# One conversion of the hidden layer is spread over three engines, and the order of all work is a new table

## The chip, the cores and the metric

The kernel runs on one core of a Trainium2 chip. The metric is the device time of one execution in microseconds (us). An execution has a span, from the first to the last instruction of the core, and a little time around it.

The core has five engines that run side by side, each with its own queue in a fixed order: TensorE (PE in the profile), VectorE (DVE), ScalarE (ACT), GpSimd (POOL) and SyncE (SP). SP issues nearly all DMAs here. An engine does nothing while the first instruction of its queue waits, so an instruction can be late because another one, ahead of it in the queue, waits for something else.

## The reference

```python
def _attn_ref(q, k, v, alpha):                 # all 4 x 8 x 768 x 48
    for t in range(S):
        state = alpha[:, :, t, :, None] * state + einsum('bhd,bhe->bhde', k[:, :, t], v[:, :, t])
        y[:, :, t] = einsum('bhd,bhde->bhe', q[:, :, t], state)

def _moe_ref(x, w_gate, w_val, w_out):         # x: 3072 x 384, hidden 1536
    g = x @ w_gate
    silu = g * (1.0 / (1.0 + exp(-g)))
    return (silu * (x @ w_val)) @ w_out
```

A gated linear recurrence over 768 steps per batch and head makes `y`; its heads side by side are the rows `x` of a gated feed-forward layer. The weights arrive in 64 bits.

## The kernel before, in words

**The recurrence** is cut into 16 units of 192 steps (4 batches x 4 units, names u = 0 to 15). For a unit, VectorE turns the loads of alpha, k and q (`tr`, `tk`, `tq`, line 399), runs a scan backwards (`G`, line 472) and one forwards (`f`, line 481), GpSimd or VectorE scale k and q (`mk`, `q`), and TensorE multiplies. From unit 4 on the products of a unit are one *burst* `Z` on TensorE: the outputs of the unit before (lines 658 to 680), the scores (line 565) and the carried state (line 584), some 3 us together. Before a burst, VectorE must have written the unit's `K` (`kr`, 16 transposes, line 540), and the unit's values must have been loaded (`V`, 8 DMAs, line 443). Behind the burst the output rows are split into two parts (`yh`, `yl`, lines 705 and 709) and ten DMAs (`xr`, line 745) lay them into `xT`, which the feed-forward reads. Units 0 to 3 are *turned* by TensorE instead (line 419).

**The feed-forward** is 96 steps: 8 blocks of 384 rows by 12 slices of 128 hidden columns. A block needs two units. TensorE keeps precision by three products of split operands, so each of a step's three parts is nine matmuls of 128x128 by 128x384: `g` and `v` (line 760), and `o` (line 793). Between them a step has a chain on the other engines: `sl`, the silu of `g`, on ScalarE (line 768); `h`, times `v`, on VectorE (line 772); `hh`, the upper part of `h`, a copy to the matmul's type on ScalarE (line 776); `hl`, the rest, `h - hh`, on GpSimd or VectorE (line 781). `g` has one PSUM bank, `v` one, and there are two buffers each of `h`, `hh` and `hl`.

Beside that the weights are converted in the first 140 us (lines 163 to 178, 343, 347), and later the weights and alpha are loaded once more for a check of their ranges (`wr`/`wc`, lines 300 and 303; `Lc`/`ck`, line 456).

**What sets the order.** The order of the whole program is written out in a table, `ORDER`, of 1637 words such as `v:h44` or `y:Lq11`: an engine (t TensorE, v VectorE, s ScalarE, g GpSimd, y SyncE) and a piece of work, for TensorE at times the PSUM banks. The last loop of `main_path` emits them in that order; each engine's queue holds its own words in it, and buffers are given out in it.

Of the kernel before, what the change touches and what calls it, by code (L numbers as in the profile page):

```python
# [49 lines left out]
t:Y0@36 s:yh0.0 y:La3 t:Ta2@20 s:pa3 s:ea2 y:Lk2 y:V1.0 s:w1a s:yh0.1 g:w1p y:Lq2 y:V1.3 y:V1.5 y:V1.2 v:w3v2 v:de1  # L50
t:S1@71 t:C1.0@2 s:ad1.0 v:yl0.0 v:ma1.2 t:Ta3@15 t:C1.1@4 s:ad1.1 t:C1.2@0 y:wl4 s:w4v0 s:ad1.2 g:pq2 g:pk2 g:vc1
v:ma1.1 v:yl0.1 v:ma1.0 t:Y1@64 s:yh1.0 v:w2v2 v:w2a s:yh1.1 t:R0.1@0 t:R0.2@3 t:Tq2@72 s:x0.2 s:x0.1 s:cq2 v:G2
v:yl1.0 v:yl1.1 t:R1.1@6 s:x1.1 v:w4v1 v:w4v2 t:Tk2@74 v:mk2 v:f2 v:q2 y:Lk3 s:pk3 t:R1.0@0 t:R0.0@6 y:V2.4 s:x0.0
s:x1.0 t:R1.2@7 s:x1.2 t:K2.0@2 s:kc2.0 g:w2p y:wl5 s:w5v0 y:V2.2 y:V2.0 y:Lq3 g:pq3 s:w4a t:Tk3@34 t:K2.1@7 s:kc2.1
t:g0 s:sl0 y:V3.1 y:V2.1 y:wl7 y:V2.3 y:V2.5 v:de2 g:vc2 g:lm0 y:V3.2 y:wl8 y:wl6 y:V3.3 y:V3.0 v:w5v1 s:ea3 v:G3
t:S2@20 s:qc2 v:ma2.2 v:mk3 v:ma2.0 v:lm1 y:wl11 y:wl9 y:V3.4 y:V3.5 s:w3a g:w3p g:w4p v:ma2.1 t:C2.0@7 t:K2.2@1
s:kc2.2 s:ad2.0 t:g1 t:v0 t:C2.1@3 v:h0 s:ad2.1 s:sl1 t:K3.0@7 s:kc3.0 t:Tq3@03 t:C2.2@1 s:ad2.2 s:cq3 s:hh0 s:w6v0
v:f3 t:v1 t:K3.1@7 t:g2 v:w5v2 g:hl0 v:h1 v:q3 v:de3 v:w6v1 s:hh1 s:kc3.1 s:sl2 t:Y2@20 s:yh2.0 v:hl1 v:w6v2 t:C3.0@4
t:S3@67 s:w5a g:w5p t:v2 s:ad3.0 t:C3.1@1 s:yh2.1 v:ma3.2 v:w8v0 v:yl2.0 s:w6a g:w6p t:o0 t:o1 v:ma3.1 v:yl2.1 y:wl12
y:La4 y:V4.5 y:wl10 s:w7v0 s:qc3 v:h2 v:ma3.0 y:xr2.0 y:xr2.1 v:w7v1 v:w7v2 v:w8v1 s:w9v0 s:ad3.1 s:vc3 t:g3 v:w8v2  # L60
v:w9v1 y:Lk4 y:wl13 y:xr2.2 t:Y3@20 s:sl3 s:w7a s:hh2 v:hl2 v:w7p s:w8a v:w8p s:yh3.0 s:yh3.1 t:v3 v:h3 s:w10v0 v:w9v2
s:hh3 v:hl3 t:g4 v:w10v1 s:sl4 s:w9a g:w9p t:o2 t:v4 v:yl3.1 v:yl3.0 v:h4 s:hh4 g:hl4 t:g5 v:w10v2 v:w10a s:w11v0
s:sl5 s:w12v0 t:v5 t:o3 v:w11v1 v:w10p t:g6 s:sl6 v:w12v1 v:w11v2 s:w11a v:h5 g:w11p s:hh5 t:o4 g:hl5 v:w12v2 y:xr3.0
y:xr3.1 y:xr3.2 y:wl16 y:V4.1 y:wl14 t:v6 v:tk4 v:h6 s:hh6 g:hl6 t:g7 v:tr4 v:G4 s:sl7 s:w13v0 s:w12a y:Lq4 v:mk4
# [1101 lines left out]
```

## Time and profile before

| | us |
|---|---|
| median of 3 runs | 547.37 (547.32 to 549.72) |
| the profiled execution | 549.81 |
| its span | 548.1 |
| TensorE busy in the span | 528.0 |
| VectorE, ScalarE, GpSimd busy | 400.5, 249.4, 151.2 |
| TensorE's granted clock | 0.999 (full speed, the 2.4 GHz level) |

The profile gives for each engine the time in which it is busy, and for an idle stretch what released it. Idle time of an engine is only worth something if TensorE's next matmul waits for it in the end. Matmuls are pipelined and their recorded ends are modelled, so TensorE's idle time is a lower bound of what it loses.

### The profile page before, as it was taken

What the parts mean: (1) busy time and instruction counts of PE and PEld (TensorE: products, weight loads), DVE (VectorE), ACT (ScalarE), POOL (GpSimd) and SP (SyncE); (2) the same over time, 40 slices, a digit from 0 to 9 for tenths busy, and PEclk for the clock granted to TensorE, in tenths of its full rate; (3) what the DMA queues carried; (4) which work ended last, traced back from release to release, by engine and by line L of the source; (5) the groups of instructions that cost most, each with busy time, mean ns of one, the idle gap of its engine ahead of it and who ended that gap; (6) DMA issues with size and microseconds to landing.
All of it is one profiled execution on the core that took longest, in us unless ns stands there. A gap on an engine that the chain in (4) does not pass through costs nothing.

```text
span 548.1 us, 13557 instructions
## 1 busy us (share of the span) xinstructions
PE 528.0 (96%) x5350; PEld 513.7 (94%) x5350; DVE 400.5 (73%) x755; ACT 249.4 (45%) x578; POOL 151.2 (28%) x149
## 2 busy tenths in 40 slices
PE   4899999999999999999989999999999999999996
PEld 3688999999999999999989999999899999999996
DVE  7999999999999998696798966889552674112122
ACT  5997655443222324533313533454533365454652
POOL 7245233545335222231313021031201030020100
PEclk9999999999999999999999999999999999999999
DMA  8989559456376547543634764255662315423511
GB/s 243 256 263 292 146 173 249 107 139 174 85 187 151 141 106 185 157 120 73 169 76 101 203 158 112 76 136 129 184 153 73 90 50 158 135 58 104 155 50 47
DMA packets 96195, 77.61 MB, mean 142 GB/s; under 512 B 33280, under 2 KB 93056, under 8 KB 96128
## 3 DMA queue, kind: packets, MB, share of 16 engines
q1 hardware_dynamic: 96048, 76.61, 52.3%
q8 instruction: 43, 0.70, 0.6%
q14 instruction: 24, 0.20, 0.1%
...
## 4 chain that ended last, share of the span: by engine, by line
PE 66%; DVE 3%; DMA 2%; SPq 1%; issue 1%; ACT 0%; POOL 0%; DVEq 0%; POOLq 0%
PE v L760 20%; PE ops L793 20%; PE g L760 20%; PE c L680 2%; PE s L565 1%; DMA L<-in_q_dram 1%; PE c L584 1%; PE y L658 1%; PE y L659 1%; DMA xT<-X 1%; SPq L745 1%; DMA V<-in_v_dram 1%; DVE h L772 0%; DVE V L629 0%; DVE K L540 0%
## 5 line engine op out<-in xcount | busy, mean ns | idle before, releaser
L760 PE MATMUL v<-xT,w 128*128 128x384 f32 x864 | 167.3, 337 | 0.6 <-DMA xT<-X 0.6
L760 PE MATMUL g<-xT,w 128*128 128x384 f32 x864 | 166.6, 336 | 0.6 <-ACT h L768 0.4
L793 PE MATMUL ops<-w,hh 128*128 128x384 f32 x576 | 158.5, 336 | 0.0
L760 PEld LDWEIGHTS v<-xT,w 128*128 128x128 f32 x864 | 150.5, 188 | 2.2 <-issue 0.9
L760 PEld LDWEIGHTS g<-xT,w 128*128 128x128 f32 x864 | 150.7, 188 | 1.8 <-ACT h L768 0.9
L781 POOL TENSOR_TENSOR hl<-h,hh 128x384 fp32r<-128x384 f32 x65 | 69.8, 1075 | 285.5 <-ACT hh L776 271.8
L772 DVE TENSOR_TENSOR h<-h,v 128x384 f32<-128x384 f32 x96 | 53.0, 552 | 89.9 <-PE v L760 61.6
L793 PEld LDWEIGHTS ops<-w,hh 128*128 128x128 f32 x576 | 105.5, 188 | 0.3
L768 ACT ACTIVATE h<-g 128x384 f32<-128x384 f32 x96 | 47.1, 490 | 119.6 <-PE g L760 101.0
L776 ACT CAST hh<-h 128x384 fp32r<-128x384 f32 x96 | 49.1, 511 | 112.0 <-DVE h L772 77.4
L793 PE MATMUL ops<-w,hl 128*128 128x384 f32 x288 | 96.8, 336 | 0.0
L540 DVE STREAM_TRANSPOSE K<-Gs 32x192 f32<-32x192 f32 x192 | 71.1, 370 | 3.3
L793 PEld LDWEIGHTS ops<-w,hl 128*128 128x128 f32 x288 | 54.0, 188 | 0.0
L347 POOL TENSOR_TENSOR w<-t,w 128x768 fp32r<-128x768 f32 (+1 forms) x15 | 27.5, 1842 | 34.4 <-ACT w L343 25.3
L781 DVE TENSOR_TENSOR hl<-h,hh 128x384 fp32r<-128x384 f32 x31 | 18.4, 594 | 22.8 <-ACT hh L776 22.7
L481 DVE TENSOR_TENSOR_SCAN AT<-AT,back 128x771 f32<-128x771 f32 x16 | 29.2, 1824 | 0.6
L606 DVE TENSOR_TENSOR X<-s,mask 64x384 f32<-64x384 f32 (+1 forms) x48 | 26.3, 551 | 3.8 <-PE s L565 3.1
L472 DVE TENSOR_TENSOR_SCAN Gs<-AT,inj 128x772 f32<-128x772 f32 x16 | 28.5, 1780 | 0.5 <-ACT AT L866 0.3
L497 POOL TENSOR_TENSOR X<-trq,AT 112x768 f32<-112x768 f32 x11 | 18.7, 1703 | 32.1 <-DMA xT<-X 11.0
L320 ACT ACTIVATE wc<-wc,wbias 128x384 f32<-128x384 f32 x36 | 23.3, 648 | 1.2
L629 DVE TENSOR_TENSOR V<-c,V 48x96 f32<-48x96 f32 x84 | 21.4, 255 | 2.8 <-ACT V L627 0.5
L893 POOL TENSOR_TENSOR Gs<-trk,Gs 128x768 f32<-128x768 f32 x9 | 15.3, 1700 | 26.0 <-DVE Gs L472 22.2
...
## 6 DMA issues: line engine op xcount, KB each, us to landing
...
```

The costliest lines, as they stand in the source:

```text
L320: nc.scalar.activation(dev, dev, AF.Relu, bias=wbias, scale=-1.0, accum_out=wviol[:, 0, i : i + 1])
L347: eng.tensor_tensor(out=lo, in0=src, in1=hi.bitcast(F32), op=ALU.subtract)
L472: nc.vector.tensor_tensor_scan(*(x.rearrange("p g t -> p (g t)")[:, ::-1] for x in (Gs, AT, inj)), 0.0, op0=ALU.mult, op1=ALU.add)
L481: nc.vector.tensor_tensor_scan(Af, Af, back[:, 1 : n + 1], back[:, 0:1], op0=ALU.mult, op1=ALU.add)
L540: nc.vector.transpose(out=bass.AP(k0.tensor, k0.offset, [k0.ap[0], (G * 2 * D, NU), (2 * D, GF), (1, 32)]), in_=Kg[j * BO + x : j * BO + x ...
L606: nc.vector.tensor_tensor(out=X[r, z, f * GF : (f + 1) * GF, :].rearrange("r g (c t) -> r g c t", c=NU), in0=sps[f][r].rearrange("r g (c t ...
L760: nc.tensor.matmul(pt, wsp[kind, f][a][:, kt * P : (kt + 1) * P], xT[blk][:, b_, kt, :], start=(n == 0), stop=(n == 3 * KT - 1),)
L768: nc.scalar.activation(h, acc.pop(("g", blk, f)), AF.Silu)
L772: nc.vector.tensor_tensor(out=h, in0=h, in1=acc.pop(("v", blk, f)), op=ALU.mult)
L776: nc.scalar.copy(out=hh, in_=acc["h", blk, f])
L781: eng.tensor_tensor(out=hl, in0=acc.pop(("h", blk, f)), in1=hh.bitcast(F32), op=ALU.subtract)
L793: nc.tensor.matmul(ops[blk][i], h[b_][:, i * P : (i + 1) * P], wsp["o", f][a], start=(first and n == 0), stop=(last and n == 2),)
```

## The change

`hh` takes an engine as an argument, and the table is another one. The number of words is the same, 1637; every matmul, load, store and check is still there.

| work (one instruction each) | before | after |
|---|---|---|
| `hh` | ScalarE 96 | ScalarE 45, GpSimd 30, VectorE 21 |
| `hl` | GpSimd 65, VectorE 31 | GpSimd 64, VectorE 32 |
| `mk` | GpSimd 9, VectorE 7 | GpSimd 6, VectorE 10 |
| `qc`, a copy of part of q | ScalarE 9, GpSimd 7 | ScalarE 7, GpSimd 6, VectorE 3 |

A few other words change their engine by one to three each (`q`, the conversions of weights, the copies of units 0 to 3). The table has one line less, so a line behind it has a number lower by one in the kernel after.

```diff
 ORDER = """
-s:first y:La0 s:pa0 t:Ta0@23 s:ea0 y:wl0 y:Lq0 s:pq0 v:w0v0 v:w0v1 v:w0v2 v:G0 v:f0 t:Tq0@03 v:q0 y:La1 s:pa1 t:Ta1@72
...
+s:first y:La0 s:pa0 t:Ta0@23 s:ea0 y:wl0 y:Lq0 s:pq0 t:Tq0@03 v:w0v0 v:w0v1 v:w0v2 v:G0 v:f0 v:q0 s:w0a v:w0p y:La1
...
-    def hidden_hi(blk, f):
+    def hidden_hi(blk, f, eng):
         hh = acc["hh", blk, f] = p2.tile([P, NB], F32R, tag="hh", name=f"hh{blk}_{f}", bufs=NH)
-        nc.scalar.copy(out=hh, in_=acc["h", blk, f])
+        (eng.copy if eng is nc.scalar else eng.tensor_copy)(out=hh, in_=acc["h", blk, f])
...
-        todo[f"hh{s}"] = lambda eng: hidden_hi(*b)
+        todo[f"hh{s}"] = lambda eng: hidden_hi(*b, eng)
```

VectorE ahead of the burst of unit 10, before. `h_7` and `h_8` are products `h` of steps 43 and 44, `trq` is the turned q of unit 11, the scan into `AT` (line 481) is `f` of unit 11, and the last row is `kr` of unit 10, for which the burst waits:

```order
307 L772 TENSOR_TENSOR h_7_3751<-h_7_3751,v_7_3753 128x384
308 L399 STREAM_TRANSPOSE trq_3791<-L_71 128x4x6x32
309 L629 TENSOR_TENSOR SE<-c_9_3480,V_81 48x96 x2
310 L629 TENSOR_TENSOR SE<-c_9_3481,V_81 48x96 x2
311 L478 RECIPROCAL back<-Gs_3708 128x4
312 L481 SCALAR_TENSOR_TENSOR AT<-AT,back 128x771
313 L482 MEMSET AT 128x3
314 L772 TENSOR_TENSOR h_8_3725<-h_8_3725,v_8_3812 128x384
315 L540 STREAM_TRANSPOSE K_104<-Gs_3282 32x3x2x32 x4
```

The same place after:

```order
309 L398 STREAM_TRANSPOSE trk_3758<-L_72 128x4x6x32
310 L771 TENSOR_TENSOR h_8_3741<-h_8_3741,v_8_3760 128x384
311 L605 TENSOR_TENSOR X_103<-s_9_3528,mask 64x384
312 L539 STREAM_TRANSPOSE K_104<-Gs_3327 32x3x2x32 x4
313 L771 TENSOR_TENSOR h_7_3780<-h_7_3780,v_7_3785 128x384
314 L780 TENSOR_TENSOR hl_7_3802<-h_7_3780,hh_7_3800 128x384
315 L539 STREAM_TRANSPOSE K_104<-Gs_3327 32x3x2x32 x4
```

The turning of q and the scan `f` of unit 11 have moved behind the last `kr` of unit 10, the row at the end of both pieces. The turning of k of unit 11 (`trk`) stands ahead of it in both, here directly in front of `h_8`.

SyncE's queue behind the output rows of unit 12, before. `V_80` are the values of unit 14, `L_72<-in_k` is k of unit 15, `wc` and `ac` are loads for the check:

```order
359 L745 DMA xT_5160<-X_102 32x2x192
360 L745 DMA xT_5160<-X_102 48x2x192 x2
361 L303 DMA wc_5172<-in_moe_w_val_dram 128x3x256
362 L443 DMA V_80<-in_v_dram 64x3x48 x3
363 L391 DMA L_72<-in_k_dram 32x4x288
364 L392 DMA L_72<-in_k_dram 32x4x256
365 L391 DMA L_72<-in_k_dram 32x4x288
366 L392 DMA L_72<-in_k_dram 32x4x256
367 L819 DMA out_dram<-ot_2_11_5177 128x384
368 L443 DMA V_80<-in_v_dram 64x3x48 x3
```

The same place after:

```order
368 L744 DMA xT_5239<-X_102 32x2x192
369 L744 DMA xT_5239<-X_102 48x2x192 x2
370 L455 DMA ac_5252<-in_alpha_dram 128x2x288
371 L442 DMA V_80<-in_v_dram 64x3x48 x5
372 L455 DMA ac_5259<-in_alpha_dram 128x2x288
373 L442 DMA V_81<-in_v_dram 64x3x48 x2
374 L390 DMA L_72<-in_k_dram 32x4x288
```

The load of k and a store no longer stand between the last values of unit 14.

GpSimd from step 33 to step 36 after (`hh_9` is step 33, `hh_11` step 35, `hh_0` step 36; before, only `hl` stands here):

```order
97 L775 CAST hh_9_3163<-h_9_3137 128x384
98 L780 TENSOR_TENSOR hl_9_3171<-h_9_3137,hh_9_3163 128x384
99 L775 CAST hh_11_3216<-h_11_3173 128x384
100 L780 TENSOR_TENSOR hl_11_3218<-h_11_3173,hh_11_3216 128x384
101 L496 TENSOR_TENSOR X_103<-trq_3241,AT 112x768
102 L780 TENSOR_TENSOR hl_1_3322<-h_1_3269,hh_1_3320 128x384
103 L775 CAST hh_0_3360<-h_0_3347 128x384
104 L780 TENSOR_TENSOR hl_0_3362<-h_0_3347,hh_0_3360 128x384
```

A step's upper part and its rest now stand one behind the other on one engine.

## Rows read from the trace of the kernel before

**Rows 1.** The stretches: length, busy time and count by engine, clock, DMA.
```profile
0.00:40.00 40.00, 29.04 (x524) 24.54 (x524) 36.31 (x57) 31.93 (x72) 20.76 (x40) 1.00 0.89 250
40.00:205.00 165.00, 164.18 (x1802) 158.50 (x1803) 158.50 (x282) 69.38 (x142) 67.36 (x51) 1.00 0.62 164
205.00:280.00 75.00, 73.24 (x632) 72.50 (x622) 58.96 (x106) 27.68 (x69) 19.53 (x18) 1.00 0.54 138
280.00:543.00 263.00, 261.41 (x2421) 258.19 (x2416) 146.56 (x311) 119.90 (x295) 43.59 (x41) 1.00 0.42 112
```

**Rows 2.** TensorE's waits, whole span: total, times, longest.
```profile
PE y L658 <- DVE h L772: 1.8, 1, 1.8
...
PE c L584 <- issue: 1.0, 1, 1.0
PE v L760 <- DMA xT<-X: 0.6, 1, 0.6
...
PE g L760 <- ACT h L768: 0.4, 1, 0.4
...
PE g L760 <- DMA V<-in_v_dram: 0.3, 1, 0.3
```

**Rows 3.** The chain of waits from 268 to 283: start, length, what.
```profile
268.09 5.75 DMA L<-in_q_dram
...
274.02 1.61 DVE trq L399
...
276.75 1.83 DVE AT L481
...
278.74 0.56 DVE h L772
...
279.34 0.26 PE y L658
```

**Rows 4.** SP's issues from 253 to 268: start, length, count.
```profile
253.28 7.40 SPq L745 DMA_DIRECT2D xT<-X  x10
...
266.55 0.54 SPq L391 DMA_DIRECT2D L<-in_q_dram  x1
```

**Rows 5.** SP's issues around 137 to 151.
```profile
137.26 6.44 SPq L443 DMA_DIRECT2D V<-in_v_dram  x8
143.81 7.63 SPq L745 DMA_DIRECT2D xT<-X  x10
```

**Rows 6.** SP's issues from 384 to 390.
```profile
384.58 0.55 SPq L391 DMA_DIRECT2D L<-in_k_dram  x1
...
386.65 0.37 SPq L819 DMA_DIRECT2D out_dram<-ot  x1
387.44 1.91 SPq L443 DMA_DIRECT2D V<-in_v_dram  x3
```

**Rows 7.** The chain of waits, whole span: matmuls of the feed-forward.
```profile
186.96 3.12 PE ops L793 x18
...
249.47 1.56 PE v L760 x9
```

**Rows 8.** Groups by line: count, busy us, mean ns, idle before.
```profile
L772 DVE TENSOR_TENSOR h<-h,v 128x384 f32<-128x384 f32 x96 | 53.0, 552 | 89.9 <-PE v L760 61.6 <-ACT h L768 11.7 <-ACT wc L320 5.7
L776 ACT CAST hh<-h 128x384 fp32r<-128x384 f32 x96 | 49.1, 511 | 112.0 <-DVE h L772 77.4 <-PE ops L793 34.4
L374 POOL CAST sel<-ident 48x48 fp32r<-48x48 f32 x4 | 4.0, 1008 | 0.2
L343 DVE CAST w<-t 128x384 fp32r<-128x384 f32 x1 | 0.5, 473 | 0.0
```

**Rows 9.** Lines 781 and 503: count, shortest, median, longest ns.
```profile
L781 POOL TENSOR_TENSOR hl<-h,hh x65: 1004/1018/2137, 47.8 to 536.6; 128x384 fp32r<-128x384 f32 x65
L781 DVE TENSOR_TENSOR hl<-h,hh x31: 525/558/1377, 51.3 to 540.5; 128x384 fp32r<-128x384 f32 x31
L503 POOL COPY X<-X x7: 502/505/841, 20.9 to 442.5; 48x384 f32<-48x384 f32 x7
```

More of the change, by code (lines that the diff above doesn't have):

```diff
@@ L50 @@
[L50 to L64, printed above, removed]
@@ new lines @@
+s:pq3 s:sl1 y:wl6 s:w6v0 t:Tq3@65 s:cq3 v:f3 g:q3 g:qc3 v:ma2.1 s:qc2 y:wl5 s:w5v0 v:ma2.0 t:K3.0@3 t:K2.2@1 t:K3.1@7
+v:ma2.2 t:v1 v:h1 s:hh0 v:hl0 y:V3.4 t:g2 s:kc2.2 s:ad2.1 t:C2.2@5 v:w5v1 s:hh1 v:w6v1 s:kc3.0 s:ad2.2 s:kc3.1 t:Y2@42
+s:yh2.0 v:hl1 v:w5v2 s:yh2.1 s:w5a g:w5p y:V3.3 y:V3.0 y:wl15 y:V3.2 y:V3.1 v:de3 v:w6v2 s:sl2 s:w6a g:w6p t:v2
+t:C3.0@7 s:ad3.0 y:wl8 v:yl2.1 v:yl2.0 t:S3@01 t:o0 s:w8v0 s:w7v0 t:o1 t:C3.1@2 t:g3 v:ma3.0 v:ma3.1 v:ma3.2 s:vc3
+s:ad3.1 v:h2 v:w7v1 v:w7v2 s:hh2 t:Y3@10 v:lm1 v:w8v1 v:w8v2 s:w7a v:w7p s:w9v0 v:w9v1 y:wl10 y:wl11 y:xr2.0 y:xr2.2
@@ new lines @@
+y:os6.2 y:V4.7 y:La5 s:ot6.0 s:hh7 s:w15v0 g:hl7 s:hh8 t:g9 s:sl9 t:v9 v:h9 v:w15v1 v:tr5 g:hl8 s:ot6.1 t:g10 s:sl10
+v:kr4.2 t:o7 g:hh9 g:hl9 s:w13a t:g11 s:sl11 g:w13p s:w14a g:w14p y:V5.0 y:Lk5 v:tk5 t:v10 t:o8 t:o9 v:h10 v:w15v2
+s:w15a s:hh10 g:hl10 y:os6.1 y:V4.6 y:V5.6 y:wl18 s:w18v0 y:wl16 y:Lq5 y:os6.0 y:wl17 y:V4.4 y:V4.3 y:V5.4 y:V5.1
+y:V4.5 y:La6 t:v11 v:G5 v:h11 s:hh11 t:g12 s:sl12 g:hl11 s:w16v0 v:kr4.0 v:w18v1 v:w16v1 t:v12 t:g13 t:o10 v:h12
+g:hh12 s:sl13 v:mk5 v:w16v2 t:o11 g:w15p g:hl12 t:v13 s:w17v0 t:g15 s:sl15 s:w16a v:kr4.3 v:kr4.1 v:h13 s:hh13
@@ new lines @@
+t:Z4@1205 s:ad4.0 v:w17v1 v:w18v2 v:w17v2 g:hl13 t:o12 t:o13 s:w18a s:w17a t:g14 s:sl14 g:w16p g:w17p y:V5.3 y:V5.2
+y:wl19 y:V5.5 s:ot13.2 s:ot13.1 y:os13.2 y:os13.1 g:qc4 v:ma4.2 v:kr5.3 v:kr5.2 v:ad4.1 v:ad4.2 v:ma4.0 t:v14 v:h14
+s:hh14 g:hl14 v:tq5 v:f5 g:q5 y:Lk6 t:g17 s:sl17 t:v15 v:h15 s:ot13.0 s:hh15 g:hl15 t:g16 s:sl16 y:os13.0 y:pl18.2
+y:wr17 y:pl18.1 y:V5.7 g:w18p s:w19v0 t:o14 v:ma4.1 v:kr5.0 v:tr6 t:v16 v:h16 s:hh16 g:hl16 t:g19 s:qc5 s:sl19 v:G6
+v:tk6 t:v17 t:o15 v:h17 s:hh17 g:hl17 t:g18 s:sl18 v:w19v1 v:kr5.1 t:Z5@20165 s:yh4.0 s:yh4.1 v:w19v2 s:w19a s:yh4.2
@@ new lines @@
+g:w19p y:Lq6 t:o16 v:de5 v:f6 v:ma5.2 v:yl4.0 v:ad5.0 v:ma5.1 t:v18 v:h18 g:hh18 g:hl18 v:ma5.0 v:ad5.1 v:yl4.2
+v:yl4.1 v:ad5.2 g:mk6 y:V6.0 y:La7 y:V6.3 y:V6.5 y:V6.6 y:V6.7 y:wr19 y:xr4.0 y:xr4.1 y:xr4.2 t:o17 t:v19 v:h19 s:hh19
+g:hl19 s:wc19 t:g20 s:sl20 v:kr6.3 t:o18 v:ot18.1 y:os18.1 v:tq6 t:v20 v:h20 g:hh20 g:hl20 t:g21 s:sl21 g:q6 y:V6.1
+y:V6.4 y:V6.2 v:kr6.2 v:kr6.1 v:kr6.0 t:v21 t:Z6@10624 s:yh5.0 v:yl5.0 s:yh5.2 s:yh5.1 t:g22 y:pl18.0 v:ot18.2
+v:ot18.0 v:h21 v:ma6.2 v:de6 v:ad6.0 t:o19 s:hh21 g:hl21 v:yl5.1 s:sl22 v:yl5.2 v:tr7 t:v22 t:o20 t:o21 t:g23 y:V7.1
@@ new lines @@
+y:Lk7 v:tk7 v:h22 s:qc6 s:hh22 g:hl22 v:G7 v:ad6.1 v:ad6.2 g:mk7 s:sl23 t:v23 v:h23 s:hh23 g:hl23 y:os18.2 y:xr5.0
+y:xr5.2 y:xr5.1 t:g24 s:sl24 t:v24 t:o22 y:Lq7 y:V7.4 y:V7.5 y:pl23.1 v:f7 v:kr7.2 v:tq7 t:o23 v:ot23.1 v:h24 g:q7
+t:g25 s:sl25 s:hh24 g:hl24 y:os18.0 y:La8 v:kr7.1 v:tr8 t:v25 v:h25 s:hh25 t:g26 s:sl26 g:hl25 y:V7.2 y:Lk8 y:os23.1
+y:V7.7 y:pl23.0 y:wr8 y:V7.3 y:V7.0 v:kr7.3 y:pl23.2 y:V7.6 t:v26 t:g27 s:sl27 v:ma6.1 v:ma6.0 v:de7 v:kr7.0
+t:Z7@10426 s:yh6.0 s:yh6.2 s:yh6.1 s:qc7 s:wc8 y:V8.3 y:V8.0 y:V8.2 y:Lq8 y:V8.1 v:yl6.0 v:h26 v:ot23.0 y:xr6.0
@@ new lines @@
+y:os23.0 y:Lc1 v:ma7.2 v:ma7.1 v:ot23.2 t:v27 t:o24 g:hh26 g:hl26 t:o25 v:h27 s:wc17 s:hh27 t:g28 v:yl6.1 v:yl6.2
+y:xr6.2 y:xr6.1 v:G8 v:tk8 g:mk8 g:hl27 v:ad7.0 v:ad7.1 y:wr26 s:sl28 t:v28 t:g29 s:sl29 t:o26 t:o27 v:h28 v:kr8.1
+s:hh28 t:g30 g:hl28 t:o28 s:sl30 y:os23.2 y:V8.5 y:V8.6 v:tq8 y:Lk9 y:V8.7 y:V8.4 s:ck1 v:kr8.2 v:f8 g:q8 v:ma7.0
+t:v29 v:h29 g:hh29 g:hl29 t:g31 s:sl31 v:kr8.0 v:kr8.3 t:Z8@02516 s:yh7.0 v:yl7.0 t:v30 v:h30 s:yh7.2 s:hh30 v:tk9
+v:ma8.2 g:hl30 y:V9.3 y:La9 y:wr35 t:o29 t:v31 v:h31 v:tr9 v:G9 t:g32 s:yh7.1 s:sl32 s:hh31 v:hl31 v:yl7.1 v:yl7.2
@@ new lines @@
+t:o30 t:g33 t:v32 v:f9 v:h32 v:hh32 t:o31 g:hl32 s:sl33 s:wc26 g:qc8 t:g35 t:v33 v:h33 g:hh33 v:mk9 v:kr9.1 v:ma8.0
+g:hl33 s:sl35 t:g34 t:v35 t:o32 t:o33 s:sl34 v:h35 g:hh35 g:hl35 y:La10 y:Lc0 y:xr7.0 y:xr7.1 y:Lq9 y:V9.6 y:xr7.2
+v:tq9 g:q9 t:v34 v:h34 v:hh34 v:hl34 t:g37 s:sl37 y:V9.7 y:Lk10 y:V9.2 s:wc35 s:ad8.0 v:kr9.2 t:v37 t:o34 t:o35 v:h37
+v:ad8.1 v:hh37 g:hl37 y:wr15 v:tr10 v:G10 v:ma8.1 t:g36 v:ot35.2 s:ot35.0 y:os35.0 s:wc15 s:sl36 t:v36 v:h36 g:hh36
+g:hl36 v:tk10 g:mk10 t:g38 s:sl38 t:v38 v:kr9.3 v:h38 v:ad8.2 s:ot35.1 t:o36 t:o37 t:g39 s:ck0 s:sl39 g:hh38 v:hl38
@@ new lines @@
+y:wr0 y:V9.0 y:wr7 y:V9.4 y:V9.5 y:La11 y:V9.1 y:Lq10 v:de9 v:f10 t:v39 v:h39 g:hh39 t:g40 s:sl40 v:kr9.0 t:Z9@21506
+g:hl39 t:o38 t:o39 s:yh8.0 v:tq10 v:yl8.0 v:qc9 s:yh8.2 s:yh8.1 s:wc7 v:yl8.2 v:ad9.0 v:yl8.1 v:ad9.1 y:V10.3 y:V10.7
+y:V10.1 y:xr8.0 t:v40 v:ma9.2 v:ad9.2 v:h40 s:hh40 g:hl40 t:g41 s:sl41 t:v41 v:h41 v:ma9.0 g:hh41 t:g42 s:sl42 g:hl41
+y:xr8.2 y:xr8.1 y:wr3 s:wc0 v:kr10.1 v:kr10.3 t:v42 t:o40 t:o41 t:g44 s:sl44 v:h42 g:q10 v:tr11 s:hh42 y:V10.0
+y:os35.1 y:Lk11 g:hl42 v:G11 v:tk11 t:v44 t:g43 s:sl43 v:h44 g:mk11 v:ma9.1 t:v43 v:kr10.2 v:h43 s:hh43 v:hl43 t:g45
@@ new lines @@
+s:sl45 v:kr10.0 y:V10.5 y:V10.2 y:V10.6 y:V10.4 t:Z10@02516 s:yh9.0 t:o42 t:o43 g:hh44 y:wr12 g:hl44 v:yl9.0 y:Lq11
+y:wr4 v:de10 s:yh9.2 s:yh9.1 v:kr11.2 v:yl9.1 v:ma10.2 s:wc4 s:wc3 s:qc10 v:yl9.2 v:ad10.0 v:ad10.1 v:ma10.1 t:v45
+t:g46 s:sl46 v:h45 v:f11 t:o44 t:v46 v:tq11 v:h46 v:hh45 g:hl45 g:hh46 t:g47 s:sl47 v:kr11.1 v:ma10.0 v:kr11.3 g:hl46
+t:v47 t:o45 t:o46 v:ad10.2 v:h47 y:V11.0 y:V11.2 y:V11.5 y:V11.6 y:xr9.1 y:V11.1 y:xr9.2 y:xr9.0 g:q11 g:hh47 g:hl47
+g:qc11 y:La12 v:kr11.0 y:V11.3 y:V11.7 y:V11.4 t:Z11@25610 y:os35.2 s:yh10.0 s:wc12 v:yl10.0 t:o47 v:de11 v:ad11.0
@@ L145 @@
+t:g90 t:o88 t:v90 s:sl90 v:h90 g:hh90 g:hl90 t:o89 t:g91 s:sl91 t:v91 v:h91 s:hh91 t:o90 t:g92 v:hl91 t:v92 s:sl92
+v:h92 v:hh92 g:hl92 t:g95 s:sl95 s:wc22 t:o91 v:hh94 v:hl94 t:v93 t:g93 s:sl93 s:ck15 v:h93 t:o92 g:hh93 v:hl93 t:v95
+t:o93 v:h95 g:hh95 t:o94 v:hl95 v:fl t:o95 t:cp@2 v:ot95.0 y:os95.0 v:ot95.1 s:ot95.2 y:os95.1 s:oz0 y:oz1 v:fg
 """
```

134 lines of the change are left out of this document (50 added, 84 removed).

## The prediction

> **What bounds the kernel now.** I read the stretches first. TensorE is busy for 164.18 of the 165 us from 40 to 205, and for 73.24 of 75 and 261.41 of 263 us in the next two stretches [rows 1]. Its work isn't touched by the change, so little can be had there: its idle time from 40 to 543 is 0.82 + 1.76 + 1.59 = 4.17 us. In the first 40 us it idles for 40.00 - 29.04 = 10.96 us, while VectorE is busy for 36.31 of the 40. Behind 543 the last rows are stored. The same stretches show who could become the next bound: VectorE, busy for 158.50 of 165 us up to 205, and far less in the last 263 us (146.56).
>
> The waits of TensorE come second. All that it waited for behind 40 us are five waits [rows 2]: 1.8 us for `h`, 1.0 that the view calls "issue", 0.6 for `xT`, 0.4 for ScalarE's `h` (the silu), 0.3 put down to a load of values; together 4.1, which agrees with the 4.17 above.
>
> Third, I followed the longest of them back through the chain of waits [rows 3]. Read it from the top: the last load of q of unit 11 is issued at 268.09 and takes 5.75 us to land; VectorE turns it (1.61), runs the scan of unit 11 (1.83), then the product `h` (0.56), and only then the burst of unit 10 begins at 279.34. Neither the load nor the scan is anything that this burst needs; they stand ahead of `h` in VectorE's queue. And the load was late because its issue, at 266.55, stood behind the ten `xT` issues of 7.40 us [rows 4]. So the waits that are left are loads that SP issues late, handed on by an engine that works in order.
>
> **The change, part by part.** The sum is made against the profiled execution, 549.81 us (span 548.1), which is 2.44 above the median of the runs shown, 547.37; the difference that I work out is then taken from the median.
>
> *The wait of 1.8.* After the change the turning of q and the scan of unit 11 stand behind the last `kr` of unit 10, so that burst no longer waits for that load: -1.8. Late next is the load of k of unit 11, which stands directly in front of `h_8` (rivals).
>
> *The wait of 1.0.* The row names no cause. I put it down to the values of unit 14: their last three issues begin at 387.44, behind four issues for k (from 384.58) and a store (386.65) [rows 6]. After, five of them follow each other and k comes behind them, so the last is issued some 387.44 - 384.58 = 2.9 us earlier, less the two `ac` loads that now stand near. -1.0; if the cause is another one, 0.
>
> *The wait of 0.6 for xT.* Between the burst of unit 12, behind which the rows of unit 11 are stored, and the first product that reads them stand six parts of a step before and seven after. Eighteen matmuls take 3.12 us [rows 7], so a part of nine takes 1.56 and the DMAs have 1.56 us more: -0.6, with 1.0 to spare.
>
> *The waits of 0.3 and 0.4.* Ten `xT` issues of unit 5 had one load of values and four of q between them and follow each other now: -0.3. Those of unit 4 stood behind eight loads of values, 6.44 us [rows 5]; three of the eight have gone behind them, 6.44 x 3/8 = 2.4 us earlier. I take the 0.4 for ScalarE's `h` as the end of that chain: -0.4.
>
> So 4.1 us go if all of it works; no reader should take that as the gain, since the order is new everywhere.
>
> *The conversions `hh`.* 51 of them leave ScalarE, 51 x 0.511 = 26 us [rows 8]. ScalarE was not a bound, and its work there ends no TensorE wait but the 0.4 above: 0. What they cost elsewhere: on VectorE the one conversion of this shape took 0.473 us [rows 8], 21 x 0.473 = 9.9 us. All but one of the 21 belong to steps from 32 on, where VectorE has room. Up to the last `kr` of unit 8, by the order, eleven other instructions leave VectorE's queue and nine come (that one `hh` among them). So VectorE's 158.50 of 165 us do not grow: 0. On GpSimd the shape doesn't occur. From below, a copy of as many elements per partition takes 0.505 (median of seven, longest 0.841) [rows 9]; from above, a conversion to the same type took 1.008 for only 48 elements [rows 8]. By the copy it is 0.5, by the conversion per element 384 / 48 x 1.008 = 8.1. I take 0.5: GpSimd's `hl` writes the same type at 1.018 [rows 9], twice a copy for two inputs, so the type alone doesn't slow it; the four conversions are among GpSimd's first work, where small ones wait for each other.
>
> Does the chain still fit? The tightest step with both parts on GpSimd is 36: two parts, 3.12 us, stand between its `v` and its `o`. `h` 0.552, `hh` 0.505, `hl` 1.018 are 2.08: 1.0 us to spare, so 0. It is covered by those two parts alone; without one of them it would cost 0.5.
>
> The row on sharing is this: a GpSimd `hl` takes 1.018 us, but up to 2.137, and one on VectorE 0.558 but up to 1.377 [rows 9]. The Trainium skill ("GPSIMD Engine Reference", Specifications) has a reason: GpSimd's way into SBUF is shared with VectorE, and they contend when VectorE reads two SBUF inputs or runs in a two-port mode. The trace agrees with it. By that rule the 30 new copies would hold VectorE for at most 30 x 0.505 = 15 us, six of them (3 us) before 205, where 6.5 us are idle; were none of that idle time usable, the sum below would end 3 us higher, without the rule it stays.
>
> *The start.* By the order VectorE has one copy out of PSUM more to do before the rows of unit 1 are split, on which the first product waits, about 0.55 like an `h` [rows 8]: +0.5, and between -1.5 and +1.5 (three such instructions either way), since 10.96 us of idle time there hang on many short waits.
>
> *New waits.* An order that is new in every place will have some that the old one hadn't. The trace can't show them. From below 0; from above as much as before, 4.1. I take two of the small kind (0.3 and 0.4): +0.7.
>
> Sum: -4.1 + 0.5 + 0.7 = -2.9. 549.81 - 2.9 = 546.9 for a profiled execution, and 547.37 - 2.9 = 544.5 for the median.
>
> **The rivals.**
>
> *The waits move.* As many late loads appear elsewhere: -4.1 + 4.1 + 0.5, so 547.9, or 547 with a start that isn't worse. For it: SP issues as much as before, and a load that is late once costs 1.8. Against: in four places I could see the cause go.
>
> *Loads in front of VectorE's work, more of them: slower.* The place is the turning of k of unit 11, in front of `h_8`, and its like in units 9 to 15. On SP the load of k stands behind the ten `xT` issues of unit 8. Those began at 253.28 [rows 4], 2.2 us behind the start of the burst of unit 9 (249.47 + 1.56 = 251.03) [rows 7], and took 7.40 us; with three issues between of about 0.5 us, four of its own, and 5.75 us to land as q's [rows 3], it lands 2.2 + 7.4 + 1.5 + 2 + 5.75 = 18.9 us behind the start of the burst. Turning it and `h_8` take 1.61 + 0.56, so 21.0. The next `v` needs the bank that `h_8` frees; the burst of some 3 us and 12 parts stand before it, 12 x 1.56 + 3 = 21.7: it fits by 0.7 us, and decides from a landing of 6.5 us. Four such waits of 1.8 would be 7.2 us: 547.37 - 4.1 + 0.5 + 7.2 = 551.
>
> *GpSimd's conversion is long.* At 8.1 us each, the 22 steps with both parts on GpSimd need 0.55 + 8.1 + 1.0 = 9.7 us before their `o`. By the order one of them has two parts there, six have three, four have four, one has five, four have six and the rest more; what is missing is 6.6 + 6 x 5.0 + 4 x 3.5 + 1.9 + 4 x 0.3 = 54 us, so 598. It begins to cost from 1.5 us. The 0.505 row speaks against it.
>
> *The change doesn't do what it says:* the 1.0 and 0.3 have other causes than I read. Then 1.3 of the 4.1 stays and the time is 545.8, inside the first case's range.
>
> **How the numbers follow.** The forecast, waits gone and few new ones, has 0.55; its own range is 541.8 (4.1 gone and 1.5 more at the start) to 546.2 (4.1 gone, 1.5 lost at the start, 1.4 of new waits). The waits move: 0.30. Loads make it slower: 0.11. The long conversion: 0.04. A measurement of this kernel can tell about 0.5%, 2.7 us, from no change: under 544.6 is faster, over 550.1 slower. The first case is split by that line at its middle, with more of it below, since its cheap end reaches far: 0.48 faster, 0.07 the same. Of the second 0.02, 0.26, 0.02. The last two are slower. Faster 0.50, same 0.33, slower 0.17. The range leaves out the last two for the most part: 541.3 to 549.8.
>
> **What would show it.** Right: no wait of TensorE for `h` or `xT` of over 0.5 us behind 40, the stretches from 40 to 543 with under 2 us of idle time, ScalarE's busy time down by about 26 us, VectorE's up by about 10, GpSimd's `hh` near 0.5 and VectorE's near 0.47. Wrong: the burst of unit 10 or the `v` before it waiting for `h` behind a turning of k; GpSimd's `hh` over 1.5 us; or a first product well behind the one of before, which would make the start more than the half us taken here.

## The result and the profile after

Four runs of the changed kernel have a median of 551.14 us (550.49 to 551.5) against 547.48 of before: a ratio of 1.0058, interval 1.0032 to 1.0084. The forecast was 544.5. Measured again on another chip, 12 executions of after beside 29 of before (e5, below), the medians are 549.35 and 549.11, the ratio 1.0003 (0.997 to 1.0035). So the change is no gain of 2.9 us; over all executions a loss of about 0.8 us is left (after 550.2 on the mean of 16, before 549.4 of 156), which the second comparison can't tell from none. One more execution of before, over 1.5% above its fastest, is left out here and below.

First the page of after: span and busy times, the granted clock in 40 slices, and one of its DMA queues (packets, MB, share).

```profile
span 548.8 us, 13574 instructions
PE 528.4 (96%) x5350; PEld 516.2 (94%) x5350; DVE 407.6 (74%) x778; ACT 229.8 (42%) x533; POOL 158.7 (29%) x171
...
PEclk9899999999999999999999999999999999999999
...
q8 instruction: 43, 0.70, 0.6%
```

ScalarE has 19.6 us less, VectorE 7.1 more, GpSimd 7.5 more. The second slice of the clock has an 8; before had only nines. The last row comes back below.

TensorE's waits after, as in [rows 2]:

```profile
PE c L583 <- issue: 1.5, 2, 1.0
PE kps L521 <- DVE X L605: 1.4, 1, 1.4
...
PE y L657 <- issue: 0.9, 1, 0.9
PE s L564 <- issue: 0.9, 1, 0.9
...
PE A L596 <- issue: 0.6, 1, 0.6
PE v L759 <- DVE h L771: 0.6, 1, 0.6
PE s L564 <- POOL X L496: 0.4, 1, 0.4
```

The `y<-h` of 1.8 is gone, and so are the waits for `xT`, for `V` and of `g` for ScalarE. But `issue` has grown from 1.0 to 3.9: time in which TensorE waited for nothing that the profile shows.

The stretches of after, as in [rows 1] but finer at the start (busy time of each engine, granted clock, DMA share, GB/s):

```profile
20.00:22.00 2.00, 1.32 (x21) 0.90 (x20) 1.98 (x3) 1.85 (x7) 1.80 (x2) 1.00 0.53 102
22.00:26.00 4.00, 3.31 (x69) 2.84 (x73) 3.87 (x8) 1.44 (x5) 0.41 (x1) 0.57 0.91 238
26.00:40.00 14.00, 12.38 (x250) 11.12 (x242) 11.73 (x21) 12.18 (x28) 7.34 (x7) 1.00 0.79 230
40.00:205.00 165.00, 163.65 (x1744) 159.53 (x1744) 155.69 (x277) 76.08 (x155) 69.34 (x59) 1.00 0.64 172
205.00:280.00 75.00, 74.54 (x835) 73.61 (x837) 59.60 (x115) 21.68 (x56) 21.59 (x22) 1.00 0.52 131
280.00:543.00 263.00, 261.25 (x2334) 258.05 (x2326) 156.75 (x332) 102.02 (x254) 47.79 (x55) 1.00 0.42 111
```

From 22 to 26 the clock is 0.57, mostly the 1.2 GHz level, after TensorE had stood idle three times between 17.0 and 22.7 (0.4, 0.6 and 1.4 us). Before kept 1.00 there in its profile. The first feed-forward product starts at 38.1 us (before 36.5) and step 12 at 104.0 (101.4). From there to TensorE's last matmul it is 439.8 us (441.7). Idle time from 40 to 543, by the stretches, is 1.35 + 0.46 + 1.75 = 3.56 us instead of 4.17. So the profiled executions show a gain of 1.9 us behind step 12 and a loss of 2.6 ahead of it.

The conversions themselves are cheap (busy, mean ns, idle time before them; the last row is by shortest, median and longest ns):

```profile
L775 POOL CAST hh<-h 128x384 fp32r<-128x384 f32 x30 | 17.3, 578 | 145.6 <-DVE h L771 93.3
L775 ACT CAST hh<-h 128x384 fp32r<-128x384 f32 x45 | 23.0, 512 | 47.5 <-DVE h L771 35.0
...
L775 DVE CAST hh<-h x21: 354/361/461, 68.7 to 532.8; 128x384 fp32r<-128x384 f32 x21
```

### The profile page after: what moved, and what is told of

Read it like the earlier page. It is cut to its first block, busy times and chain, and to the rows that moved or that the text cites. A ratio compares the mean times of both kernels' runs of the same rounds, so it can differ in the third digit from the quotient of the medians.

```text
span 548.8 us, 13574 instructions
## 1 busy us (share of the span) xinstructions
PE 528.4 (96%) x5350; PEld 516.2 (94%) x5350; DVE 407.6 (74%) x778; ACT 229.8 (42%) x533; POOL 158.7 (29%) x171
## 4 chain that ended last, share of the span: by engine, by line
PE 91%; DVE 3%; DMA 2%; issue 1%; POOL 1%; ACT 1%; SPq 0%; DVEq 0%; POOLq 0%; ACTq 0%
PE v L759 26%; PE ops L792 26%; PE g L759 26%; PE s L564 2%; PE pt L418 2%; PE c L679 2%; PE y L657 1%; PE y L658 1%; PE c L583 1%; DMA wc<-in_moe_w_out_dram 1%; PE y L679 1%; PE A L596 1%; PE kps L521 1%; DMA xT<-X 0%; DMA V<-in_v_dram 0%
## 5 line engine op out<-in xcount | busy, mean ns | idle before, releaser
L780 POOL TENSOR_TENSOR hl<-h,hh 128x384 fp32r<-128x384 f32 x64 | 67.7, 1058 | 163.8 <-ACT hh L775 88.9
L775 POOL CAST hh<-h 128x384 fp32r<-128x384 f32 x30 | 17.3, 578 | 145.6 <-DVE h L771 93.3
L775 ACT CAST hh<-h 128x384 fp32r<-128x384 f32 x45 | 23.0, 512 | 47.5 <-DVE h L771 35.0
L346 POOL TENSOR_TENSOR w<-t,w 128x768 fp32r<-128x768 f32 (+1 forms) x14 | 24.4, 1755 | 32.4 <-ACT w L342 27.6
L496 POOL TENSOR_TENSOR X<-trq,AT 112x768 f32<-112x768 f32 x12 | 20.4, 1698 | 24.5 <-ACT K L526 8.6
(123 smaller groups left out, 551.5 us busy)
```

The source lines that it names most:

```text
L346: eng.tensor_tensor(out=lo, in0=src, in1=hi.bitcast(F32), op=ALU.subtract)
L775: (eng.copy if eng is nc.scalar else eng.tensor_copy)(out=hh, in_=acc["h", blk, f])
L780: eng.tensor_tensor(out=hl, in0=acc.pop(("h", blk, f)), in1=hh.bitcast(F32), op=ALU.subtract)
```

## The experiments

Each was timed in five rounds beside before on the same chip; before had a mean of 549.1 to 549.8 on these five occasions. "Full clock" below means an execution whose mean granted clock was 0.998 or more: 96 of the 156 of before (mean 548.5; the others 550.8) and 1 of the 16 of after.

**Start or rest, order or engines (e1 to e4, e8).** e1 is before unchanged. e2 takes the words of before's table up to `t:g6` (step 6, about 73 us) and then after's, e3 the reverse; e4 is after with `s:hhN` for every `hh`, e8 before with after's engines of `hh`:

```diff
-v:hh3 ... g:hh12 ...             # e4
+s:hh3 ... s:hh12 ...
-s:hh3 ... s:hh12 ...             # e8
+v:hh3 ... g:hh12 ...
```

e1: 

> The kernel before, unchanged, profiled and timed once more. Its four timed runs lie at 547.3 to 547.6 three times and at 549.7 once, and the profiled execution (549.81) belongs to the longer kind. Theory A (the extra 2.2 to 2.4 us of the longer kind come from the first 60 us, where loads and the clock vary): if this profile is one of about 547.4, its first feed-forward product starts about 2 us earlier than the 36.5 us of the profile shown, and the rest keeps its distances within 0.5 us. Theory B (a late load in the middle): the first product is at 36.5 as before and the difference lies in one place behind 60 us.

e2: 

> The table of before up to the first half of step 6 (about 73 us), then the table of after with its engines of hh. Theory A (the loss is made in the start: there the changed kernel's granted clock falls to 0.55 to 0.60 between 22 and 26 us, and its step 6 stands 3.1 us later): 546 to 547.5, no slower than before. Theory B (the loss is made by new waits in the middle, or by the conversions on GpSimd and VectorE): 550 to 551.5, like the changed kernel.

e3: 

> The reverse: the table of after up to the first half of step 6, then the table of before, hh on ScalarE there. Theory A (the start): 550 to 551.5, with the clock below 0.7 for some us between 20 and 27 us. Theory B (middle or conversions): 547 to 548.

e4: 

> The changed kernel with every hh on ScalarE again, the order untouched. If the conversions on GpSimd and VectorE cost (hl of GpSimd 1.06 us behind an hh of 0.58 us): 547.5 to 549. If they cost nothing and the loss is the order's alone: 550.5 to 551.5. If they do relieve ScalarE, as is meant (26 us of it): above 551.5.

e8: 

> The order of before, with each hh on the engine that it has in the changed kernel (GpSimd 30, VectorE 21). The prediction costed the conversions at nothing beside other work: 548 to 551, like before. If the place in the order matters as it did the other way round (the changed order with all hh on ScalarE took 569.5 against 549.8): 555 to 570, since hh then waits behind VectorE's and GpSimd's own queues.

e1 ran from 546.5 to 553.1 us. Its profile (550.8 span) was not of the short kind that theory A speaks of, but its extra 2.7 us lie in the start too: it has the first product at 40.8 us, 4.3 later than the profile shown ahead, with the clock at 0.72 from 10 to 22. Its waits of TensorE from 60 us on are these:

```profile
PE y L658 <- DVE h L772: 1.6, 1, 1.6
PE c L584 <- issue: 0.7, 1, 0.7
PE g L760 <- ACT h L768: 0.4, 1, 0.4
```

Neither the 0.6 for `xT` nor the 0.3 for `V` is there. In two later profiles with before's order (e14 and e18) the same places have 0.25 for `V` and 0.16 for `xT`: these waits come and go with the execution.

e2: 549.37, ratio 1.0003 (0.9978 to 1.0028), 11 of 12 at full clock. e3: 552.39, ratio 1.0044 (1.0017 to 1.0072), 1 of 12. So the start of after brings the lowered clock with it; that half of theory A held. The times don't part start from rest, since both kernels pay where the two tables meet: from step 6 to step 12 before takes 28.7 us and after 28.2, but e2 29.8 and e3 31.0. In e3's profile the clock stayed at 1.00 and the first product starts at 36.2 us, no later than before's. e2's expected 546 to 547.5 failed: after's rest, as e2 ran it, showed no gain.

e4: 569.45 (ratio 1.0357). e8: 560.29 (1.0194). The largest waits of each from 60 us on, first e4:

```profile
PE g L759 <- ACT h L767: 7.4, 5, 3.0
PE y L657 <- DVE h L771: 2.0, 1, 2.0
PE s L564 <- DVE h L771: 1.6, 1, 1.6
```

and e8:

```profile
PE ops L793 <- POOL hl L781: 3.3, 3, 2.1
PE y L658 <- DVE h L772: 1.5, 1, 1.5
PE ops L793 <- DVE hh L776: 0.9, 1, 0.9
```

In e4 `sl` waits behind an `hh` on ScalarE; in e8 `o` waits for conversions queued behind VectorE's and GpSimd's work. Order and engines belong together: either half of the change alone costs 2 to 4%.

**After again, and idle stretches filled (e5 to e7).** e6 and e7 add transposes of the identity, which nothing reads, where TensorE stood idle in the start:

```diff
+            for _ in range(n):
+                nc.tensor.transpose(t_, ident, ident)
...
-s:pq0 t:Tq0@03
+s:pq0 t:D0@5 t:Tq0@03
```

e5: 

> The changed kernel, unchanged, beside before on the same chip. Of 41 executions of before 24 had a mean clock of 0.998 or more (548.7 us on average) and 17 less (551.4); the four of after all had less. Theory A (the change makes the lowered clock of the start more frequent, and nothing else costs): most executions below 0.998, a mean of 1 to 1.5 us above before's, and the few at full clock level with before's 548.7. Theory B (new waits behind the start cost): at full clock it is still 2 us or more above 548.7. Theory C (the difference of 3.7 us was mostly the draw of few executions): the interval includes 1.

e6: 

> Before with 22 additional 128x128 transposes of the identity on TensorE into a free PSUM bank, in three of its idle stretches of the start (10 at 6.6 us, 8 at 12.9, 4 at 19.2; nothing reads them). If idle TensorE in the start is what the clock falls after: nearly all executions at 0.998 or more and the median falls from 549.8 to about 548.5. If the clock falls for another reason: the same mix of clocks, and 549.8 or, where the transposes delay the next products, up to 1 us more.

e7: 

> The changed kernel with 28 such transposes (8 at 6.7 us, 8 at 12.8, 4 at 18.5, 8 at 21.3, the stretches in which its TensorE stood idle). If idle TensorE in the start is what the clock falls after: most executions at 0.998 or more, and 1 to 1.5 us less than the changed kernel. If not: the clock as without them, and the time the same or up to 1 us more.

e5: ratio 1.0003, 1 of 12 at full clock: theory C for the size, theory A for the clock. Its profile, stretches as above:

```profile
22.00:26.00 4.00, 3.35 (x69) 2.88 (x72) 3.87 (x8) 1.38 (x5) 0.37 (x1) 0.57 0.87 241
26.00:32.00 6.00, 3.98 (x136) 3.30 (x127) 4.99 (x8) 5.16 (x13) 4.55 (x5) 1.00 0.92 251
32.00:40.00 8.00, 6.49 (x79) 6.01 (x80) 2.50 (x4) 2.74 (x7) 2.11 (x3) 0.57 0.30 81
```

The same fall at 22, and a second one behind a `y<-issue` of 2.9 us at 30.5. e6 (551.79, ratio 1.0028) and e7 (549.23, ratio 1.002) gained nothing; 8 and 4 of 12 at full clock. Both failed their expectation, and their traces had `issue` stops in new places, which led to the next question.

**Stops at fixed places of the queue (e9 to e11).** This is the stop in the `y` of burst 1 and that in the `c` of burst 14, after (start, duration, operation, idle time before it):

```profile
30.44 0.22 PE L658 MATMUL y<-X,V 112*48 112x64 f32 x1
31.60 0.27 PE L657 MATMUL y<-X,V 128*64 128x64 f32 x1 [0.94 <-issue]
...
394.20 0.47 PE L583 MATMUL c<-V,K 64*48 64x48 f32 x18
395.69 0.48 PE L583 MATMUL c<-V,K 64*48 64x48 f32 x25 [1.02 <-issue]
```

and the latter place in before:

```profile
393.41 0.46 PE L584 MATMUL c<-V,K 64*48 64x48 f32 x19
394.89 0.56 PE L584 MATMUL c<-V,K 64*48 64x48 f32 x29 [1.02 <-issue]
```

The `c` stops in the middle, behind its 18th or 19th matmul, on nothing. I counted TensorE's recorded instructions (weight loads, matmuls, semaphores) up to each stop where neither neighbour waits for a semaphore. After stops at places 704, 1472, 5568 and 8640 (start to start 1.16, 1.12, 0.67 and 1.23 us), before at 8640 (1.23), e6 at 4800, 8128 and 9664, e7 at 704, 4800 and 8128. All are 192 more than a multiple of 256 (to one or two, as one counts), and at the other such places 0.2 us at most is lost. The page's row of the instruction queue fits: 43 packets, 0.70 MB, so 16 KB each, and TensorE's 10,815 instructions are 42.2 times 256. A stop came where the 256 instructions ahead had been used up within 2.2 us (a burst's small matmuls), in the first 60 us, with the queues full of loads, within 4.6 or so; but not behind each such block (before's at 5568 was used up in 2.1 us, and nothing was lost).

The times of this queue's packets, kept in the traces, show what a stop waits for. Each block of 256 has its packet. In before the one for the block at 8640 moved from 392.54 to 393.49 us, and TensorE went on at 394.89; in after from 393.11 to 394.42, and it went on at 395.69. Taking blocks and packets in order, 56 gaps of more than 0.25 us at such places in the 20 traces end 1.2 to 1.7 us (median 1.4) behind the end of the block's own packet (13 others, with other causes, 2 to 24 us behind it), and nowhere did TensorE pass such a place sooner than 1.2 us behind it. By this, after's gap of 0.47 at 8128, beside a semaphore, is a stop too. Before's block at 5568 had its packet by 250.48, 3 us ahead. So a stop comes where TensorE reaches a block before the block's instructions have come; a short block ahead makes that likely, not certain.

If so, instructions added at the start move every later stop. e9 to e11 add matmuls of one element there:

```diff
+                nc.tensor.matmul(t_[0:1, 0:1], ident[:, 0:1], ident[:, 0:1], start=True, stop=True)
```

e9: 

> The changed kernel with 66 one-element matmuls (nothing reads them) in two idle stretches of TensorE in the start, 33 at 6.7 us and 33 at 12.8: they move every later instruction of TensorE's queue 132 places on. Theory F (instruction supply: where neither instruction waits for anything, TensorE stood still only at places 704, 1472, 4800, 5568, 8128, 8640 and 9664 of its queue, all 192 more than a multiple of 256, and only where the 256 instructions ahead were used up in under 2.3 us, or under 4.8 us in the first 60): the four stops of the changed kernel (704, 1472, 5568, 8640; 4.2 us in its profile) are gone, two new ones stand at 6336 (at about 278 us) and 7616 (340 us), about 1.2 us each: 1.5 to 3 us faster than the changed kernel. Theory G (those stops belong to the work there: the y of burst 1, the scores of unit 3, the c of units 10 and 14): they stay, and the time with them.

e10: 

> Before with 42 such matmuls (21 at 6.6 us, 21 at 12.9). Theory F: by the same rule stops at 4288, 4800 and 8128 for sure, and at 704, 7616 and 9664 on the edge, in the place of the one at 8640: 2 to 5 us slower than before. Theory G: as before, within 0.5 us.

e11: 

> Before with 12 such matmuls (6 and 6): a control of the same build. Theory F: one stop, at 8128 (369 us) in the place of 8640 (394 us), so the time of before within 0.5 us. If the added matmuls themselves cost or save: a difference to before here too.

One such matmul is recorded as two, so the shifts were 132, 84 and 24 and the places expected for e9 to e11 are wrong. Counted with the true shift, the rule gives for e11 4800, 8128 and 9664: its trace stops just there (1.07, 1.36, 0.32), and no longer at 8640. For e10 it gives 1728, 3264, 3776, 6336 and on the edge 7616: the trace has the first four (1.14, 1.43, 2.63, 0.93). For e9 only places on the edge: the trace has no stop in a burst, but 0.35 and 0.48 from start to start at 5056 and 8384, where 0.17 is usual, behind blocks of 3.0 and 2.6 us. Two of e11's three, in the same view:

```profile
204.86 0.90 PE L584 MATMUL c<-V,K 64*48 64x48 f32 x43
206.62 0.29 PE L584 MATMUL c<-V,K 64*48 64x48 f32 x5 [0.87 <-issue]
...
369.67 0.65 PE L584 MATMUL c<-V,K 64*48 64x48 f32 x35
371.47 0.39 PE L584 MATMUL c<-V,K 64*48 64x48 f32 x13 [1.15 <-issue]
```

and the longest of e10:

```profile
163.01 0.55 PE L584 MATMUL c<-V,K 64*48 64x48 f32 x31
165.97 0.42 PE L584 MATMUL c<-V,K 64*48 64x48 f32 x17 [2.42 <-issue]
```

Theory G falls: the work at 394 us is the same in e11 and doesn't stop. Times: e10 553.16 (1.0078, 1.0049 to 1.0106), e11 551.09 (1.0047, 1.0022 to 1.0072), slower as their stops ask. But e9, with only some 0.5 us lost in stops, took 549.7 (1.0017): 0 of 12 at full clock.

**Stops and clock together (e12 to e18).** These set shift and filling apart: 20 transposes at 12.8, 18.5 and 21.3 us in after (e12, e17; 21 in e16; 12 at the latter two places in e13), with one-element matmuls at 6.7 us for the shift in all but e17 (e13 has some at 12.8, 17.0 and 22 as well); 9 transposes at 12.9 and 19.2 in before (e14, e18); 5 at 12.9 in e2's kernel (e15).

e12: 

> The changed kernel with the same shift of 66 matmuls, 46 of one element at 6.7 us and 20 transposes of 128x128 in the later idle stretches (8 at 12.8 us, 4 at 18.5, 8 at 21.3), after which the clock fell at 22 us. If both the stops and the lowered clock are what the start costs: the stops as in the first kernel of this call, the clock at 0.998 or more in most executions, 546 to 548, faster than both kernels. If the clock does not follow TensorE's idle time: like the first kernel.

e13: 

> The changed kernel with 122 matmul places filled in five idle stretches of its start: 46 one-element ones at 6.7 us, 50 at 12.8, 14 at 17.0, 12 at 22 (a written one takes two places, as the runs before showed), and 12 transposes of 128x128 at 18.5 and 21.3: a shift of 134 matmuls. Theory F with the clock: no stop for instructions in the whole program (the nearest blocks, at 5824 and 8896, are used up in 2.2 us), the clock at 0.998 or more in nearly all executions as in the run of shift 112, and 546.5 to 547.5: faster than before's 549.1 to 549.8. If the stops are made up for elsewhere (work that waits in the same place anyway): 548 to 549.

e14: 

> Before with 9 transposes of 128x128 in two idle stretches of its start (5 at 12.9 us, 4 at 19.2). Theory F: the stop at 8640 is gone and no other comes (5568 is on the edge): 1 us less than before at the same clock, 547.5 to 548.5 on the mean of the executions at 0.998 or more. If the c of unit 14 waits for something of its own, as the prediction put it: the wait at 394 us stays, and the time is that of before.

e15: 

> The kernel with the start of before up to step 6 and the rest of after, with 5 transposes at 12.9 us: the stop at 1472 (1.06 us in the profile without them) goes, those at 5568 and 8640 are on the edge of going. Theory F: 1 to 2 us less than without the shift (549.4 to 549.8): 547.5 to 548.5. If stops do not reach the end: 549.5 as without.

e16: 

> The changed kernel with a shift of 67 matmuls: 46 one-element ones at 6.7 us, 9 transposes at 12.8, 4 at 18.5, 8 at 21.3. By the rule of the places: no stop in the first 60 us, two later ones, at 6336 (278 us) and 7616 (340 us), about 1 us each. If a stop in the start and TensorE's idle stretches of 18 to 23 us are what lowers the clock: 0.998 or more in nearly all executions and 547 to 548.5. If the clock does not follow them: the mix of the changed kernel, 549 to 551.

e17: 

> The same 20 transposes less one at 12.8 us (8, 4, 8) and nothing at 6.7 us: a shift of 20. By the rule the stop at 704 (30 us) stays, with new ones at 4800, 8128 and 9664 in the place of 1472, 5568 and 8640. If the stop in the start lowers the clock by itself: mostly below 0.998, 549.5 to 551. If the idle stretches alone do: mostly 0.998 or more, 548.5 to 549.5.

e18: 

> The kernel before with 9 transposes at 12.9 and 19.2 us, once more on another chip. It had 548.3 on average against 549.2 of before (ratio 0.998, 0.9955 to 1.0005), all twelve at 0.998 or more. If that is its worth: again nearly all at 0.998 or more and 0.5 to 1.2 us less than before. If it was a draw: the mix of before, and the same time.

The stops that were counted ahead with the true shift mostly came: e16's at 6336 and 7616 (1.16 and 1.31 from start to start) and e17's at 704, 4800 and 8128 (0.98, 1.14, 1.23), but none at e17's 9664. Others came unexpected: in e16 at 960 (0.87, at 31 us) and 3264 (0.79). e12, expected to stop like e9, has them at 1728, 5824 and 8896 (0.73, 0.96, 0.67).

The order of after, with full-clock executions and mean time:

| | stop at 704 (28 to 30 us) | no stop at 704 |
|---|---|---|
| idle at 18.5 and 21.3 us | after 1 of 16, 550.2 | e9 0 of 12, 550.0 |
| filled there | e7 4 of 12, 549.9; e17 5 of 12, 551.9 | e12 12 of 12, 548.4; e16 9 of 12, 548.7; e13 7 of 12, 550.3 |

Filling the idle stretches keeps the clock in more executions: e9 and e12, timed side by side, have 0 and 12 of 12. What the stop does to it is not shown. The filled kernels with a stop at 704 have fewer executions at full clock, but e13 and e16 have a stop at 960 instead, 29 and 31 us from the start, and in the profiles of e7 and e17 the clock stays at 1.00 behind the stop at 704. e13 was expected without any stop; its trace has five, at 960, 1728, 5056, 8384 and 9920 (0.5 to 1.0 from start to start): a miss. The stretches from 22 us on, first of e9:

```profile
22.00:26.00 4.00, 2.63 (x38) 2.16 (x42) 3.88 (x7) 2.05 (x7) 1.02 (x2) 0.57 0.92 273
26.00:40.00 14.00, 13.33 (x268) 12.20 (x263) 11.55 (x18) 11.20 (x26) 7.34 (x7) 0.88 0.73 203
```

and of e12, where the clock stays:

```profile
22.00:26.00 4.00, 3.68 (x132) 3.20 (x130) 3.87 (x8) 2.44 (x8) 1.22 (x3) 1.00 0.90 254
26.00:40.00 14.00, 13.01 (x210) 11.51 (x201) 13.36 (x22) 13.02 (x31) 8.44 (x7) 1.00 0.87 254
```

Ratios to before: e12 0.9992 (0.9972 to 1.0011), e13 1.0026, e15 1.0008, e16 0.9987 (0.9967 to 1.0007), e17 1.0037 (1.0009 to 1.0065). e15's time is within 0.6 us of e2's: expected 1 to 2 less, a miss.

e14 and e18, before with nine idle transposes: 0.998 (0.9955 to 1.0005) and 0.9978 (0.9956 to 1.0001), 21 of 24 at full clock, mean 548.3 against 549.4. The stop of unit 14 is gone in e14, but a new one, not expected, stands at 8128 (0.89 from start to start):

```profile
367.40 0.44 PE L793 MATMUL ops<-w,hh 128*128 128x384 f32 x1
368.40 0.34 PE L793 MATMUL ops<-w,hl 128*128 128x384 f32 x1 [0.56 <-issue]
...
392.46 0.75 PE L584 MATMUL c<-V,K 64*48 64x48 f32 x48
393.14 0.44 PE L793 MATMUL ops<-w,hh 128*128 128x384 f32 x1
```

All 48 matmuls of `c` run in one piece, 0.75 us, with the loads of unit 14 where they were. e18 and e15 have such new stops too, at 4800 and 8128 (0.4 to 0.7). e14's kernel is the best version tried, about 1 us under before; both intervals just include 1, and among executions at full clock it is 0.3 to 0.4 under before's, so most of it is the clock. Filled in the same way, the changed order (e12, e16: 548.55 on 24 executions) is not faster than the old one (548.3). Their stops are not alike (three and five in the profiles of e12 and e16, one and two in those of e14 and e18), so what the changed order would do without them is not shown.

## Why the prediction was wrong, point by point

- **The `c` of unit 14, -1.0, failed.** I read its 1.0 of `issue` as a wait for the last values. It is a stop for instructions at place 8640, which both tables reach in the same `c`; it stayed (1.23 us start to start in both) and went with nine transposes more (e14), which moved 8128 to the end of another burst, where a new stop stands. The Trainium skill ("Runtime: NRT & Kernel Launch", Instruction fetch mechanics) says that instructions come in blocks of 256 and that crossing a block is mostly hidden. These traces show the 256, and most crossings cost nothing; they cost up to 2.6 us where the packet's end was less than some 1.4 us ahead.
- **The start, +0.5, was mis-sized.** It is +1.6 to the first product and +2.6 to step 12. The term held copies on VectorE alone, and so did its bound of 1.5; the clock, 0.57 from 22 to 26, was not in it. Where the clock stays (the profiles of e7, e12, e16 and e17) the same order has the first product at 36.6 to 36.9 us (before 36.5) and step 12 at 101.4 to 102.3 (101.4). Where it falls without a stop at 704 (e9), the first product is at 39.0. What the stops at 704 (1.16) and 1472 (1.12) add is not shown: e7 and e17 have the former. My own sign of error, a first product well behind, came true.
- **Burst 10, -1.8, and `g`, -0.4, held:** both waits stand in e1 too, and neither in after nor in e5. But the former was only 0.4 in e14, with before's order, so it is not the same in every execution either. The 0.6 and the 0.3 come and go with before's order: e1 has neither, e14 0.25 of the latter, e18 0.16 of the former. Of the 4.1, the 2.2 of the first two waits stood in both profiles of before.
- **New waits, +0.7:** 0.6 (`v<-h`) and 0.4 (`s<-X`) and a stop of 0.67 at 5568, which no term held. The 0.6 is one late load more, as in the rival that the waits move: a load of `wc` lands at 376.1 us, ScalarE converts it ahead of `yh`, VectorE's `yl` waits for that, and `h` stands behind it until 378.5. From 60 us on TensorE's waits went from 4.1 to 2.5 (from 2.7 in e1 to 1.4 in e5): a gain of 1.3 to 1.6 instead of 3.4. In the profiled executions it is 1.9 from step 12 on, and the 2.6 lost ahead of it turn the sum of -2.9 into +0.7. My sign of being right, under 2 us of idle time from 40 to 543, failed with 3.56.
- **The conversions, 0, held in the new order:** 0.578 us on GpSimd (0.505 taken), 0.361 the median on VectorE (0.473), ScalarE -19.6 instead of -26 (its 45 `hh` take 26 less, other work came to it). None of TensorE's waits after is for `hh` or `hl`. What the Trainium skill says of the shared way into SBUF ("GPSIMD Engine Reference", Specifications) cost nothing that shows: VectorE was busy 155.7 us from 40 to 205, 2.8 less than before with five instructions fewer, and an `h` took 0.553 us on the mean (0.552). What I hadn't priced is that they are what makes this order possible (e4, 18 us).
- **The base.** The profiled 549.81 was one draw of a kernel that takes 546.4 to 554.1, and the median of 547.37, from which 544.5 was worked out, lies 2 us under the mean of 549.4. Four runs of either kernel can't tell 3 us: the 0.0058 of the first comparison became 0.0003 with 12 executions beside 29.
- **The rivals.** That causes were misread was priced at 545.8, faster still; I hadn't joined it with a worse start. Loads in front of `h_8` didn't occur, nor the long conversion.

Open: what decides the clock of before. e6 and e11, in whose profiles the clock stays in the start, were at full clock in only 8 and 4 of 12. And before's executions at full clock still spread over 5 us (546.4 to 551.9).
